# One core, a retention layer and a wave-MLP: the whole program behind the first loads in another order

## The chip, the cores and the metric

The kernel runs on one core of a Trainium2 chip. The metric is the device time of one execution in microseconds (us). The kernel before takes 165.86 us, the median of 3 runs (165.68 to 165.93). The core's engines are told apart by the names that the profile gives them: PE (TensorE, with PEld for its weight loads), DVE (VectorE), ACT (ScalarE), POOL (GpSimd), and SP (SyncE), which here only issues DMAs. Each engine takes its instructions from its own queue, in program order.

## The reference

For 4 batches, 8 heads, 768 tokens and a head size of 64 the first half is a recurrence with a decay gamma per head. Its output, laid out as 4 x 768 x 512, is the input of the second half.

```
state = gamma * state + k[t] (outer) v[t]          # per batch and head, 64 x 64
x[t]  = (q[t] @ state) / sqrt(64)
theta = x @ w_theta                                # 512 x 512
y     = w_tok_r @ (x * cos(theta)) + w_tok_i @ (x * sin(theta))   # 768 x 768, per batch
u     = x + y
out   = u + max(u @ w_ch, 0)                       # 512 x 512
```

All tensors in memory are 32 bit; the kernel multiplies in bf16.

## The kernel before, in words

The recurrence is done in blocks. A unit n (0 to 23) is 256 tokens of 4 heads of one batch: six units to a batch, units n and n+1 (n even) being the two head groups of the same tokens. A chunk C or t (0 to 23) is 128 tokens of all heads, six to a batch. The second half needs all six chunks of a batch, since w_tok_r and w_tok_i mix tokens.

There are no loops in the program's order. A text, ORDER (lines 22 to 86), is a list of tokens such as `Lk.4.a`: a step, a unit or chunk, at times a second index, and where there is a choice the engine or queue (`v` DVE, `a` ACT, `p` POOL, `s` SP). The last loop of the kernel (line 603) calls the steps one by one. The list alone fixes the order in every engine's queue. Semaphores between the engines, and the buffers that a tile gets, come from the framework. Loads, stores and transposes that SP and ACT issue are counted in program order on eight semaphores in turn, so that such a DMA is not issued before the one eight places ahead of it has landed.

The steps of a unit n:

- `Lk`, `Lq`, `Lv` (line 157): load k, q or v of the unit, 256 KB each, from SP's or ACT's queue. There are 16 buffers for k and q together and 9 for v.
- `ck`, `cq` (lines 137, 139): cast k or q to bf16. `cqs` (302) does the cast of q and multiplies by the decay of its token at once; where `cq` is used, the decay comes in later, in `XA`. `cv` (308): cast v, with its decay.
- `Tk`, `Tq` (316): transpose k or q on PE, four blocks each, into PSUM; `E` (137, 139) copies both to SBUF. `Dk` (332) does the same by a DMA transpose that SP issues.
- `A` (346): the products of q and k, on PE; `m` (355): mask them, on DVE.
- `ST` (373): the unit's addition to the state, on PE; `S0`, `S1` (391, 395): add it to the running state; `SB` (139, 137): cast the state to bf16, in two halves.
- `I` (411) and `Y` (423): the state's and the products' part of the output, on PE, into the two PSUM banks R0 and R1 in which the next unit's `ST` also writes. There is one buffer of each, so `I` of unit n waits until `S0`, `S1` and both `XB` or `XA` before it have been read out.
- `XB` (137, 139): copy a chunk's half of the output as bf16 to the tile xT. `XA` (441): the same on DVE, multiplied by the decay qx.

The steps of a chunk: `Tx` (455) and `Ex`, or `Dx` (462): transpose xT to x, on PE with a copy or by DMA. `Hh` (469): theta. `CN` (476): cosine and sine, on ACT. `z` (483): x times both, on DVE or POOL. `M.t.s` (509): the two products of token block s for output chunk t, two matmuls of 512 columns. `u` (516): add x. `Tu` (521) and `Eu`, or `Du` (531): transpose u. `O` (536): the last product. `f` (542): relu and add. `SO` (547): store. `Mh`, `uh`, `Tuh`, `Euh`, `Oh`, `fh`, `SOh` do the last chunk in two halves.

The weights: `Pth`, `Pch` and `Pw.r.g` (173, 176, 182) load them from POOL's queue, w_tok in three groups of rows each (1, 2 and 3 blocks). `Tw`, `Ew` (491, 137, 139) transpose w_tok. `const1` to `const9` make the constants; `const9` and `const8` are eight activations on ACT for qx (line 233), the later 512 and the first 256 tokens. `Z` (278) is a pair of matmuls on zeros.

Of the kernel before, what the change touches and what calls it, by code (L numbers as in the profile page):

```python
# [39 lines left out]
Tu.0 I.7 cv.8.p E.8.a cv.9.p Y.7 ST.8 A.8 cqs.9.v ck.9.v M.2.4 Du.1 Lk.10.s Eu.0.a XB.7.1.a XB.7.0.v  # L40
S0.8.v SB.8.0.v M.2.2 Tx.6 Tq.9 Tk.9 Lv.10.a cv.10.p ck.10.p Lq.10.s S1.8 u.2 m.8 O.0 E.9.a SB.8.1.a
Hh.6 Tw.1.4 I.8 Y.8 A.9 CN.6.0 Du.2 Lq.14.s CN.6.1 Ex.6.v f.0 ST.9 Tw.0.3 Hh.7 Ew.1.4.v Ew.0.3.a
S0.9.v Tw.0.4 M.3.0 Tw.1.5 CN.7.0 CN.7.1 M.3.2 Dx.7 M.3.1 M.3.5 M.3.3 Lv.12.s Lk.12.s Ew.1.5.v
XA.8.1 Ew.0.4.v Lq.12.s M.3.4 u.3 S1.9 Tw.0.5 Tk.10 M.4.5 cqs.10.p XA.8.0 m.9 M.4.3 Tq.10 SB.9.1.a
SB.9.0.a I.9 O.2 Lq.11.s Lk.11.s E.10.a Lk.15.s Ew.0.5.v Lk.14.s Y.9 ST.10 A.10 z.7.p Lv.11.s
# [588 lines left out]
```

## Time and profile before

| what | value |
|---|---|
| median of 3 runs | 165.86 us (165.68 to 165.93) |
| span of the profiled execution, first to last instruction | 164.0 us, 4889 instructions |
| PE busy | 153.7 us, 94% |
| DVE busy | 113.1 us, 69% |
| ACT busy | 79.6 us, 49% |
| POOL busy | 76.9 us, 47% |
| moved by DMA | 34.93 MB, mean 213 GB/s |

The page gives no other time for the profiled execution than its span; the 1.9 us between the span and the median of the runs lie outside the first and the last instruction. Busy time is an average over stages of unlike limits, and PE's end times are modelled. Rows of the views read: start in us, length in us, engine, line, operation, tiles written and read, and in brackets how long the engine sat idle before and what ended that. In grouped rows the figures behind the bar are the busy time in us and the mean length of one in ns.

### The profile page before, as it was taken

To read this page: it belongs to the slowest core of one execution; us is meant where nothing else is said; L and a number is where in the kernel's file an instruction comes from. 1 tells how busy PE (TensorE), PEld (TensorE's weight loads), DVE (VectorE), ACT (ScalarE), POOL (GpSimd) and SP (SyncE) were. 2 spreads that over 40 slices of the span, in tenths; PEclk is the share of its full clock that TensorE was granted. 3 is DMA by queue.
4 is the path that set the end of the run, shared out by engine and by line. 5 is a ranking of instruction groups with operands and counts; after the bars stand their busy time and mean duration, and the time that the engine had idled before them with its cause. 6 is when DMAs were issued, how large, how long until landed. Compare 5 with 4: busy or idle time off the path is not lost.

```text
span 164.0 us, 4889 instructions
## 1 busy us (share of the span) xinstructions
PE 153.7 (94%) x2001; PEld 87.0 (53%) x2030; DVE 113.1 (69%) x210; ACT 79.6 (49%) x142; POOL 76.9 (47%) x109
## 2 busy tenths in 40 slices
PE   5997789999999999999999999999999999999992
PEld 1455556656666655654454565555555545455550
DVE  3298677977993896994879895789867760244462
ACT  4976889983658245762433725832341616000020
POOL 7957279186306733730307599951469104500000
PEclk9999999999999999999999999999999999999999
DMA  4999999999999999949999896999999438514455
GB/s 118 297 290 251 272 284 250 279 217 280 210 214 257 290 170 222 310 115 285 318 259 199 173 247 182 187 169 301 213 271 131 96 83 211 160 68 123 104 209 203
DMA packets 69062, 34.93 MB, mean 213 GB/s; under 512 B 26416, under 2 KB 66096, under 8 KB 69040
## 3 DMA queue, kind: packets, MB, share of 16 engines
q1 hardware_dynamic: 56032, 23.73, 67.4%
q10 hardware_dynamic: 10320, 7.47, 16.1%
q0 software_dynamic: 2688, 3.41, 12.1%
q8 instruction: 16, 0.26, 0.7%
q14 instruction: 6, 0.05, 0.1%
HBM read 25.69 MB, written 6.29 MB: 195 GB/s over the span
## 4 chain that ended last, share of the span: by engine, by line
PE 73%; DMA 12%; ACT 5%; POOL 4%; issue 2%; DVE 1%; DVEq 0%; SPq 0%; POOLq 0%; ACTq 0%
PE y_ps L509 35%; PE o_ps L536 12%; PE th_ps L469 9%; DMA row<-in_moe_w_tok_i_dram 5%; DMA kqf<-in_k_dram 4%; DMA kqf<-in_q_dram 4%; PE r_ps L423 3%; ACT qx L233 3%; PE at_ps L346 2%; PE r_ps L411 2%; PE kq_ps L316 2%; PE w_ps L491 2%; PE y_ps L561 2%; PE r_ps L373 1%; PE u_ps L521 1%
## 5 line engine op out<-in xcount | busy, mean ns | idle before, releaser
L509 PE MATMUL y_ps<-z,wti 128*128 128x512 bf16 x131 | 49.6, 379 | 1.0 <-issue 1.0
L509 PE MATMUL y_ps<-z,wtr 128*128 128x512 bf16 x131 | 49.7, 379 | 0.3
L483 POOL TENSOR_TENSOR z<-cs,x_sb 128x1024 bf16<-128x1024 bf16 x12 | 25.4, 2124 | 17.6 <-DMA x_sb<-xT 10.0
L355 DVE TENSOR_TENSOR at<-at_ps,mask 128x1024 bf16<-128x1024 f32 x24 | 29.2, 1216 | 0.6 <-PE at_ps L346 0.5
L308 POOL TENSOR_TENSOR vb<-vf,vsc 128x512 bf16<-128x512 f32 x17 | 18.0, 1063 | 21.3 <-DMA vf<-in_v_dram 21.0
L542 DVE SCALAR_TENSOR_TENSOR ot<-o_ps,u 128x512 f32<-128x512 f32 x23 | 15.8, 688 | 12.9 <-PE o_ps L536 12.8
L469 PE MATMUL th_ps<-wth,xT 128*128 128x512 bf16 x88 | 23.9, 379 | 0.5
L516 DVE TENSOR_TENSOR u<-y_ps,x_sb 128x512 bf16<-128x512 f32 x23 | 15.8, 688 | 12.0 <-PE y_ps L509 11.9
L536 PE MATMUL o_ps<-wch,uT 128*128 128x512 bf16 x88 | 23.2, 379 | 0.4 <-issue 0.2
L476 ACT ACTIVATE cs<-th_ps,zerob 128x512 bf16<-128x512 f32 x24 | 16.4, 684 | 12.7 <-PE th_ps L469 8.2
L476 ACT ACTIVATE cs<-th_ps,halfpi 128x512 bf16<-128x512 f32 x24 | 16.3, 684 | 10.5 <-issue 4.3
L139 POOL CAST sbd<-s 64x256 bf16<-64x256 f32 (+1 forms) x21 | 10.0, 476 | 22.9 <-DVE s L391 20.5
L509 PEld LDWEIGHTS <-wtr 128*128 128x128 bf16 x138 | 13.5, 98 | 12.7
L509 PEld LDWEIGHTS <-wti 128*128 128x128 bf16 x138 | 13.5, 98 | 11.9 <-DVE wti L139 0.2
L137 ACT COPY kqT<-kq_ps 128x1024 bf16<-128x1024 bf16 x12 | 12.1, 1012 | 10.9 <-PE kq_ps L316 10.9
L137 ACT CAST kqb<-kqf 128x512 bf16<-128x512 f32 x17 | 10.2, 619 | 8.0 <-DMA kqf<-in_k_dram 7.2
L469 PEld LDWEIGHTS <-xT 128*128 128x128 bf16 x96 | 8.9, 98 | 8.3
L536 PEld LDWEIGHTS <-uT 128*128 128x128 bf16 x92 | 8.4, 98 | 8.6
L316 PE MATMUL kq_ps<-ident,kqb 128*128 128x128 bf16 x120 | 11.2, 219 | 0.4 <-ACT kqb L137 0.2
L278 PE MATMUL zz<-zero 128*128 128x512 bf16 x27 | 9.5, 481 | 2.0 <-DVE zero L192 1.9
L423 PE MATMUL r_ps<-at,vb 64*64 64x128 bf16 x384 | 10.0, 221 | 1.1 <-DVE at L355 1.1
L316 PEld LDWEIGHTS <-kqb 128*128 128x128 bf16 x120 | 8.2, 98 | 4.5 <-POOL kqb L139 0.6
(77 smaller groups left out, 204.6 us busy)
## 6 DMA issues: line engine op xcount, KB each, us to landing
vf<-in_v_dram SPq DMA_DIRECT2D x20, 256.0 KB, 6.0
kqf<-in_k_dram SPq DMA_DIRECT2D x19, 256.0 KB, 5.3
kqf<-in_q_dram SPq DMA_DIRECT2D x17, 256.0 KB, 5.1
out_dram<-ot ACTq DMA_DIRECT2D x12, 256.0 KB, 3.0
out_dram<-ot SPq DMA_DIRECT2D x11, 256.0 KB, 3.1
kqf<-in_q_dram ACTq DMA_DIRECT2D x7, 256.0 KB, 5.4
kqf<-in_k_dram ACTq DMA_DIRECT2D x5, 256.0 KB, 5.0
vf<-in_v_dram ACTq DMA_DIRECT2D x4, 256.0 KB, 6.1
```

Source lines behind the costliest of these rows:

```text
L137: nc.scalar.copy(dst, src)
L308: engines[e].tensor_mul(in_blocks(vb), by_token(raw["vf", n]), _bcast_last(K["vsc"][:, i, :, h * HU:(h + 1) * HU], D))
L316: nc.tensor.transpose(st["kq_ps", n][:, 4 * w + x, :], st["kqb", n][:, w, x * P:(x + 1) * P], K["ident"])
L355: nc.vector.tensor_mul(at.rearrange("p g j a t -> p (g j) (a t)"), st["at_ps", n].rearrange("p g j a t -> p (g j) (a t)"), _bcast_mid(K["m ...
L423: nc.tensor.matmul(st["R", n + 1][c][g * D:(g + 1) * D, j * P:(j + 1) * P], st["vb", n][rows, lo:lo + D], st["at", n][rows, g, j, a, :], s ...
L469: nc.tensor.matmul(th_ps, st["xT", C][:, j, :], K["wth"][:, j, :], start=(j == 0), stop=(j == 3))
L476: nc.scalar.activation(st["cs", C][:, w, :], st["th_ps", C], AF.Sin, bias=K["zerob" if w else "halfpi"], scale=1.0)
L483: engines[e].tensor_mul(st["z", b][:, c], st["cs", C], _bcast_mid(x_of(C), 2))
L509: nc.tensor.matmul(st["y", t], K["wT"][r][:, s0, t0 * P:(t0 + 1) * P], st["z", b][:, s0, r, :], start=(done == 0 and r == 0), stop=(done = ...
L516: nc.vector.tensor_add(st["u", t], st["y", t], st["x", b][:, t0, :])
L536: nc.tensor.matmul(o_ps, st["uT", t][:, j, :], K["wch"][:, j, :], start=(j == 0), stop=(j == nD - 1))
L542: nc.vector.scalar_tensor_tensor(st["ot", t], st["o", t], 0.0, st["u", t], ALU.max, ALU.add)
```

## The change

Only ORDER is changed. The first 17 tokens (constants, the first five loads) stay as they are. Behind them nearly every step stands in another place, although units and chunks are still worked off in the same succession. What else differs:

- Casts and copies. `E` on DVE goes from 3 to 7 of 15, on ACT from 12 to 8. `z` on DVE goes from 12 to 16 of 24, on POOL from 12 to 8. q is scaled in its cast in 16 units instead of 13 (`cqs`), so that `XA` falls from 22 to 16 and `XB` rises from 26 to 32; but units 0 to 3, which had `cqs`, now have `cq` and `XA`. `ck` goes on DVE from 5 to 2, on POOL from 7 to 9, on ACT from 12 to 13. `Ew` has 8 on DVE (9) and 4 on ACT (3).
- Queues. Of 72 loads ACT issues 30 (16 before) and SP 42 (56 before); of the stores ACT issues 11 in place of 12, the last half chunk aside.
- Transposes. Chunk 8 has `Dx` for `Tx` and `Ex`, and `Du` for `Tu` and `Eu`. As the diff has it these are two transposes more by DMA; the nine `Dk` are the same.
- In the first part: `Lk.1` goes from SP to ACT's queue, behind `const9`. `Lq.4`, `Lk.4` are issued ahead of `const8` instead of behind it, `Lv.5` by ACT. `Pw.1.0`, `Pw.0.0`, `Pw.0.1`, `Pw.1.1` follow on POOL behind `ck.5` and `cv.5`, with no `z` between them.

The diff, cut to its beginning (up to `M.1.1`) and its end:

```diff
 ORDER = """
-const2 Lv.0.s const1 const6.v Z.29 Z.2 const5 Z.38 Lk.0.a const3 Z.35 Z.8 Lq.0.s Lv.1.s Z.28 constA
-const4 Lq.1.a cqs.0.v const9 Lk.1.s cv.0.p Z.39 const8 ck.0.p Tk.0 Tq.0 ck.1.a E.0.v Lq.4.a ST.0
-Lk.4.a Z.15 A.0 cqs.1.p Tq.1 Lq.2.s S0.0.v SB.0.1.v Lk.2.s SB.0.0.p cv.1.p Lv.2.s S1.0 I.0 Z.27 m.0
-Tk.1 E.1.a Y.0 ST.1 XB.0.1.a cqs.2.v Z.34 S0.1.v S1.1 cv.2.p SB.1.0.a Pth Lq.3.s Z.18 XB.0.0.v Tq.2
-A.1 SB.1.1.a ck.2.a Tk.2 const7 I.1 Z.23 m.1 Y.1 XB.1.0.a Lk.3.s E.2.v XB.1.1.v A.2 ck.3.p m.2 ST.2
-S0.2.v S1.2 SB.2.1.a Z.11 cqs.3.p Tq.3 Lv.3.s Tx.0 Tk.3 Z.3 ck.4.p Lv.4.s Lk.5.s Lq.5.s Lv.5.s
-Lq.6.s Lk.6.s Lv.6.s Lq.7.s E.3.a SB.2.0.v I.2 Y.2 XB.2.1.a Ex.0.a cv.3.v cq.4.p Tk.4 Lq.8.s A.3
-ST.3 Lk.7.s S0.3.v SB.3.0.a S1.3 Lv.7.s Lk.8.s Tx.1 Tq.4 SB.3.1.p cv.4.p m.3 Pw.1.0 XB.2.0.a Ex.1.a
-I.3 Lv.8.s E.4.a cq.5.a Y.3 Pw.0.0 ST.4 Hh.0 ck.5.a S0.4.v XB.3.0.v XB.3.1.v cv.5.v CN.0.1 A.4
-CN.0.0 Tq.5 Hh.1 Tk.5 SB.4.0.p SB.4.1.a Pw.0.1 Hh.2 m.4 E.5.v I.4 Y.4 ST.5 ck.6.a Tk.6 Tx.2 cq.6.a
-CN.1.1 CN.1.0 XA.4.1 A.5 XA.4.0 m.5 Lq.9.s Ex.2.v S0.5.v z.0.p Tq.6 E.6.a CN.2.0 cv.6.p Hh.3
-SB.5.0.v Tx.3 Tw.1.0 z.1.v SB.5.1.a Ew.1.0.v Ex.3.a CN.2.1 A.6 I.5 Y.5 ST.6 XA.5.0 z.2.v Tw.0.0
-CN.3.0 Tx.4 CN.3.1 Ew.0.0.v S0.6.v XA.5.1 Ex.4.v Hh.4 CN.4.0 CN.4.1 Tw.0.1 M.0.1 Pw.1.1 z.3.v M.0.0
-Tw.0.2 Pw.1.2 Ew.0.2.a SB.6.1.a Hh.5 z.4.p SB.6.0.p Lk.9.a M.0.3 ck.7.p cqs.7.p M.0.2 CN.5.1 CN.5.0
-cq.8.a m.6 Ew.0.1.v Tw.1.1 Tw.1.2 Ew.1.1.v Lv.9.s M.0.4 M.1.0 Tx.5 Ew.1.2.v M.1.1 S1.6 Tk.7 M.1.4
...
-M.20.5 u.20 O.22 Mh.1.5 uh.1 f.22 Tu.20 SO.14.a SO.19.s Eu.20.a O.21 SO.18.a Tuh.1 Euh.1 f.21 O.20
-f.20 Oh.0 Oh.1 SO.21.a SO.22.s SO.20.s fh.0 SOh.0 fh.1 SOh.1 Z.31
+const2 Lv.0.s const1 const6.v Z.29 Z.2 const5 Z.38 Lk.0.a const3 Z.35 Z.8 Lq.0.s Lv.1.s Z.28 constA const4
+Lq.1.a cq.0.v const9 cv.0.p cq.1.v ck.0.p Tk.0 Lk.2.s Lk.1.a Tq.0 Z.18 ST.0 Z.39 Lq.4.a Lq.2.s E.0.v Lv.2.s
+Lq.5.s S0.0.v Lk.3.s A.0 Tq.1 SB.0.1.v cv.1.v Lk.4.a const8 ck.1.a Lv.3.s Tk.1 S1.0 Lq.3.s ck.2.a SB.0.0.v
+Z.15 Lv.4.s Lk.5.s m.0 I.0 cq.2.a Y.0 cv.2.p Pth E.1.v XA.0.1 A.1 cqs.4.v ST.1 Tk.2 Z.3 cq.3.p S0.1.v Z.34
+Tq.2 m.1 ck.4.a E.2.v Lq.6.s XA.0.0 Tq.4 ck.3.a cq.5.p A.2 Z.27 SB.1.0.v S1.1 SB.1.1.a I.1 m.2 cv.3.p Y.1
+const7 ST.2 Lk.7.s XA.1.0 cv.4.p ck.5.p S0.2.v Tk.3 XA.1.1 Tk.4 Tq.3 Z.11 S1.2 Lk.6.s Z.23 E.3.v A.3
+SB.2.0.a Lv.5.a Tx.0 SB.2.1.a I.2 Y.2 E.4.v ST.3 Tx.1 m.3 S0.3.v Ex.1.v Lq.7.s Tq.5 XA.2.1 Pw.1.0 XA.2.0
+Lv.6.s SB.3.1.a S1.3 SB.3.0.a A.4 cv.5.p I.3 Y.3 ST.4 Pw.0.0 Hh.0 m.4 CN.0.0 Ex.0.v XA.3.0 Pw.0.1 XA.3.1
+S0.4.v Tk.5 CN.0.1 E.5.v Tx.2 Ex.2.v Pw.1.1 Hh.1 SB.4.0.a CN.1.0 SB.4.1.v Lq.8.s Hh.2 I.4 ck.6.p Y.4 ST.5
+cqs.6.v Tq.6 Lk.8.s A.5 z.0.v CN.1.1 Hh.3 S0.5.v SB.5.1.a SB.5.0.a Tk.6 CN.2.1 Tw.1.0 XB.4.0.v XB.4.1.v I.5
+m.5 Pw.1.2 E.6.a cv.6.v Lv.7.a Y.5 A.6 ST.6 z.1.v CN.2.0 Ew.1.0.a XA.5.0 Tw.0.0 Tx.3 Ew.0.0.v z.2.p Ex.3.v
+CN.3.1 m.6 Hh.4 S0.6.v CN.3.0 Tx.4 M.0.0 z.3.p Tw.0.2 M.0.1 Lk.9.a Ex.4.a Lv.9.a Ew.0.2.v CN.4.1 M.0.2
+Lk.10.a Tw.0.1 SB.6.0.a CN.4.0 XA.5.1 ck.7.p Ew.0.1.a Tx.5 Lv.10.a z.4.v Ex.5.a Lv.8.s S1.6 Hh.5 Tw.1.1
+CN.5.0 CN.5.1 SB.6.1.p M.0.4 Tw.1.2 cq.7.p M.0.3 Ew.1.1.v Tk.7 I.6 z.5.v Ew.1.2.a M.1.0 cv.7.v Tq.7 E.7.a
+Lq.9.s M.1.1 cqs.8.p M.1.2 M.0.5 Lk.18.a M.1.4 Pch Tq.8 Y.6 Pw.0.2 A.7 ST.7 ck.8.v u.0 Tw.1.3 Tk.8 S0.7.v
...
+Mh.1.4 M.20.1 Mh.1.3 Tuh.0 f.18 M.20.2 Du.21 M.20.0 u.20 O.22 Mh.1.5 Tu.20 SO.18.s Euh.0 f.22 uh.1 Eu.20.a
+O.21 SO.16.a Tuh.1 f.21 Euh.1 SO.22.a O.20 SO.21.a Oh.0 Oh.1 f.20 Z.31 SO.20.a fh.0 fh.1 SOh.0 SOh.1
 """.split()
```

More of the change, by code (lines that the diff above doesn't have):

```diff
@@ L40 @@
[L40 to L45, printed above, removed]
@@ new lines @@
+M.8.4 M.8.1 XB.13.1.v Lq.21.a cv.15.v S0.14.v Dk.16 M.8.0 cqs.18.p Lq.19.s XB.13.0.a Lv.20.s SB.14.1.p
+Lk.19.a M.8.2 Hh.13 CN.13.0 Dk.17 u.8 Tx.12 S1.14 M.10.0 M.10.4 SB.14.0.p M.10.5 Du.7 CN.13.1 I.14 Hh.12
+SO.4.s Y.14 m.15 ST.15 A.16 S0.15.v M.10.3 XB.14.0.v S1.15 SB.15.1.p CN.12.0 M.10.2 CN.12.1 Lk.21.s
+XB.14.1.v O.6 ck.20.a M.10.1 Dx.13 SB.15.0.p I.15 Y.15 m.16 ST.16 ck.21.a A.17 f.6 cqs.20.p u.10 O.7 S0.16.v
+XB.15.0.v Dk.18 M.11.1 Lv.19.s XB.15.1.v cv.18.p ck.19.p SB.16.1.a Tx.15 M.11.3 Du.10 Ex.12.a SB.16.0.a I.16
```

76 lines of the change are left out of this document (36 added, 40 removed).

## The prediction

> **What bounds the kernel now.** I read the page's engine table first, then the same by stages, then the chain of waits of the first 40 us, and only then single instructions. The table:
>
> ```profile
> PE 153.7 (94%) x2001; PEld 87.0 (53%) x2030; DVE 113.1 (69%) x210; ACT 79.6 (49%) x142; POOL 76.9 (47%) x109
> ```
>
> PE is the bound on average. The stages (start and end in us, length, then each engine's busy time) and two matmuls of `M` in a row say where:
>
> ```profile
> 5.00:30.00 25.00, 22.09 (x427) 13.91 (x434) 18.15 (x35) 20.54 (x37) 17.54 (x23) 1.00 1.19 272
> 25.00:30.00 5.00, 4.78 (x108) 3.27 (x111) 3.92 (x9) 4.77 (x8) 4.12 (x4) 1.00 1.14 256
> 32.00:160.00 128.00, 125.72 (x1529) 70.39 (x1551) 90.66 (x165) 54.22 (x98) 55.62 (x56) 1.00 0.94 203
> ...
> 36.36 0.38 PE L509 MATMUL y_ps<-z,wtr 128*128 128x512 bf16 x1
> 36.58 0.38 PE L509 MATMUL y_ps<-z,wti 128*128 128x512 bf16 x1
> ```
>
> The columns behind the length are PE, PEld, DVE, ACT and POOL, then the granted clock, which is full. From 32 us on PE is busy 125.72 of 128 us, and its matmuls of 512 columns start 0.22 us apart: there it does nothing but its work, and an order can hardly win. From 5 to 30 us PE is busy 22.09 of 25 us, in pieces that often wait for one another, and DVE, ACT and POOL are at 70 to 82%; from 25 to 30 all four are near full. So the change is decided in the first 32 us, and by what it makes PE wait for later. The chain of waits shows what sets the front:
>
> ```profile
> 5.47 3.38 ACT qx L233 x6
> 9.27 6.62 DMA kqf<-in_k_dram
> 15.91 0.37 SPq L157
> 16.32 5.75 DMA kqf<-in_q_dram
> 24.53 1.17 POOL z L483
> 25.70 0.91 issue
> 26.61 0.98 POOL vb L308
> 27.60 8.04 DMA row<-in_moe_w_tok_i_dram
> ...
> 37.39 0.22 PE x_ps L455 x4
> 44.07 0.22 PE u_ps L521 x4
> ```
>
> ACT computes qx; only then does it reach `Lk.4.a`, at 9.27; the DMA eight places behind it, SP's `Lk.5`, may not go before that lands, at 15.91; q of unit 5, its casts, the cosine and `z.0` on POOL follow, and behind `z.0` and `cv.6` POOL asks for the weights `Pw.1.1`, at 27.60.
>
> **The change part by part.** *PE.* `Tx.8` and `Tu.8` go, two groups of four transposes at 0.22 each in the chain: **-0.45 us**, all of it on the path, since PE is dense there. Their copies `Ex.8` (DVE) and `Eu.8` (ACT) go too, into idle time. In their place SP issues `Dx.8` and `Du.8`, whose landing takes:
>
> ```profile
> uT<-u SPq DMA_TRANSPOSE x16, 3.2
> x_sb<-xT SPq DMA_TRANSPOSE x12, 3.6
> kqf<-in_k_dram ACTq DMA_DIRECT2D x5, 256.0 KB, 5.0
> ```
>
> In the new order PE has 15.9 us of work between the last `M.8` and `O.8`, counting each step by its pieces in the chain (0.43 for an `M`, 0.86 for `Hh` and `O`, 0.22 for four transposes). A transpose of 3.2 us hides there. If SP were late by 12 us it would not; in SP's queue `Du.8` stands right behind `Du.10`. `Dx.8` stands behind `Dk.12`, with 17 us of PE's work up to the first `M` that needs it.
>
> *Loads.* ACT issues 14 loads more. The nearest row is an issue beside a running copy: the copy begins at 33.81, the issue at 33.82, and the next copy at 34.63 without a pause.
>
> ```profile
> 33.81 0.80 ACT L137 COPY wtr<-w_ps 128x768 bf16<-128x768 bf16 x1 [0.36 <-PE w_ps L491]
> 33.82 0.38 ACTq L157 DMA_DIRECT2D kqf<-in_k_dram  x1
> 34.63 0.29 ACT L137 CAST sbd<-s 64x128 bf16<-64x128 f32 x1
> ```
>
> So I take 0; were each on the path it would be 14 x 0.38 = 5.3 us, and ACT has 84 us idle. The one that counts is `Lk.1`. It went out from SP's queue early enough that `ck.1` at 8.79 waited for ACT alone; now ACT reaches it when the last of `const9`'s four activations has begun.
>
> ```profile
> 8.79 0.62 ACT L137 CAST kqb<-kqf 128x512 bf16<-128x512 f32 x1
> 3.96 4.89 ACT L233 ACTIVATE qx<-pos,lscale,lgp 128x512 f32<-128x512 f32 x8 [0.43 <-POOL lgp L228]
> L233 ACT ACTIVATE qx<-pos,lscale,lgp 128x512 f32<-128x512 f32 x4 | 2.9, 802 | 0.4 <-POOL lgp L228 0.4
> 12.13 0.39 PE L316 MATMUL kq_ps<-ident,kqb 128*128 128x128 bf16 x4
> 12.92 1.23 DVE L355 TENSOR_TENSOR at<-at_ps,mask 128x1024 bf16<-128x1024 f32 x1 [0.36 <-PE at_ps L346]
> ```
>
> That is 3.96 + 2.9 - 0.8 = about 6.1. It lands some 5.0 later, at 11.1; `ck.1` on ACT takes 0.62 (to 11.7), `Tk.1` 0.39 (12.1), and `E.1`, now on DVE, 0.68 (12.8). Nothing on DVE passes `E.1`: behind it wait `XA.0.1`, `cqs.4` and `S0.1`, 1.2 together, and then `m.1`, at 14.0. In the kernel before `m.1` began at 12.92.
>
> *Casts and copies in the first units.* Through `m.5` DVE has 45 instructions in place of 30: three `E`, four of `XA` and `XB`, three `Ex`, two `cq`, two `SB`, one `z` and one `S0` more, one `cv` less. Their rows, and three instructions in a row that show the spacing:
>
> ```profile
> L139 DVE COPY kqT<-kq_ps 128x1024 bf16<-128x1024 bf16 x3 | 2.1, 684 | 1.2 <-PE kq_ps L316 1.2
> L137 ACT COPY kqT<-kq_ps 128x1024 bf16<-128x1024 bf16 x12 | 12.1, 1012 | 10.9 <-PE kq_ps L316 10.9
> L441 DVE TENSOR_TENSOR xT<-r_ps,qx 128x256 bf16<-128x256 f32 x22 | 8.7, 416 | 1.8 <-PE r_ps L373 1.8
> L139 DVE CAST kqb<-kqf 128x512 bf16<-128x512 f32 x6 | 2.9, 501 | 0.0
> L483 DVE TENSOR_TENSOR z<-cs,x_sb 128x1024 bf16<-128x1024 bf16 x12 | 8.2, 682 | 0.2
> 22.95 0.69 DVE L308 TENSOR_TENSOR vb<-vf,vsc 128x512 bf16<-128x512 f32 x1
> 23.56 1.22 DVE L355 TENSOR_TENSOR at<-at_ps,mask 128x1024 bf16<-128x1024 f32 x1
> 24.69 0.68 DVE L139 COPY kqT<-kq_ps 128x1024 bf16<-128x1024 bf16 x1
> 27.17 1.22 DVE L355 TENSOR_TENSOR at<-at_ps,mask 128x1024 bf16<-128x1024 f32 x1
> 29.57 0.40 PE L411 MATMUL r_ps<-kqT,sbd 128*128 128x128 bf16 x4
> ```
>
> By length: 3 x 0.68 + 7 x 0.42 (`Ex` as long as `XA`) + 2 x 0.50 + 2 x 0.3 + 0.68 + 0.3 - 0.69 = 6.9 (0.3 stands for the small casts and sums of the state, after the one of 0.29 on ACT above); an instruction follows the one before it 0.08 earlier than that one's length (22.95 to 23.56), so 15 x 0.08 less: **5.7 us** more. ACT loses three `E` of 1.01 in the same part. From `m.1` at 14.0 up to `m.5` the new queue holds 31 instructions, by the spacing 4 x 1.13 (`m`) + 4 x 0.60 (`E`) + 12 x 0.34 (`XA`, `XB`, `Ex`) + 9 x 0.2 (states) + 2 x 0.60 (`cqs`, `z`) = 14.0. If DVE never waited, `m.5` would begin at 28.0, where it began at 27.17 before: 0.8 later. If it waited as much as before, 5.7 later. It idled 6.85 of the 25 us from 5 to 30, and this would shrink to 1.1. I take it that DVE, with more work ready, keeps about a third of the 4.9 us between these ends, so that `m.5` comes 0.8 + 1.5 = 2.3 us later. Some 1.2 of this is slack: `m.5` was done at 28.4, and `I.5` and `Y.5` behind it only began at 29.57. What is left is **+1.1 us** (from 0 to 4.5) at the place where PE gets dense.
>
> *POOL.* It does four `z` fewer, and `Pw.1.1` stands ahead of both its `z`. But `Pw.0.0` to `Pw.1.1` stand behind `cv.5`, whose load ACT issues behind `SB.2.0`. I put this between 2 us for and 1 us against, and take 0, since PE was already busy 4.78 of 5 us before the rows came.
>
> *After 32 us.* DVE stays some 5 us ahead in work, of 37 that it idles there; POOL hands it four more `z`. I take **+0.3** for waits on `m` and `u` (0 to 1.5). One more matter is contention between DVE and POOL:
>
> ```profile
> 86.72 2.03 POOL L308 TENSOR_TENSOR vb<-vf,vsc 128x512 bf16<-128x512 f32 x2
> 87.20 2.10 DVE L302 TENSOR_TENSOR kqb<-kqf,qsc 128x512 bf16<-128x512 f32 x1
> L302 DVE TENSOR_TENSOR kqb<-kqf,qsc 128x512 bf16<-128x512 f32 x6 | 5.6, 931 | 3.2 <-DMA kqf<-in_q_dram 3.2
> ```
>
> Six `cqs` took 5.6 us, 1.5 more than six of the 0.68 that I take for an undisturbed one; one beside POOL's `cv` took 2.10. From 39 instructions of DVE on SBUF alone the new order goes to 42, so this costs 0.1 more; it lies within the +0.3. [...]
>
> Sum, against the profiled span of 164.0: +1.1 - 0.45 + 0.3 = +0.95, so 164.95; with the 1.86 us by which the median of the runs (165.86) stands above this span, **166.8 us**.
>
> **The rivals.** *Faster.* `Lk.4` now goes out ahead of `const8`, whose four activations take 4.89 - 2.9 = 2.0, so some 2.0 before 9.27; the chain's pieces from `z.0` to `cv.6` (1.17 + 0.91 + 0.98) no longer stand before `Pw.1.1`; and ACT, 4.77 of 5 us busy from 25 to 30, is freed. If the front is set by this chain and DVE's waits were only its shadow, the front moves 2.0 earlier and the time is 165.86 - 2.0 - 0.45 = 163.4. It decides if `m.5` begins before 27.2. Against it: DVE cannot reach `m.5` before 28.0 by its own work, unless `E.1` comes earlier than 12.1.
>
> *DVE becomes the bound of the front.* If it keeps all its waits, `m.5` is 5.7 later and the front 4.5: 165.86 + 4.5 - 0.45 = 169.9. Speaking for it: its waits come from PE and loads in turn. Against: part of its idle time is waiting for `E` copies that ACT took 1.01 for and DVE takes 0.68 for.
>
> *No difference.* The front's delay is eaten by the slack before `I.5`, and only the transposes count, with some later waits: 165.5 to 166.2.
>
> **How the numbers follow.** I call a difference under 0.2% (0.33 us) none, about what a measurement here can tell. Forecast, later front by 0.5 to 2.5 us net: 0.42. DVE as the bound, above 168.4: 0.13. No difference: 0.13. Faster, 163.2 to 165.5: 0.32. So faster 0.32, same 0.13, slower 0.55. The likeliest case's own range is 166.2 to 168.4. The range for 8 in 10 takes in most of the faster case and the milder part of the DVE case: 164.0 to 168.8.
>
> **What would show it.** Right: `Lk.1` issued at about 6.1 and `E.1` on DVE past 12; `m.1` near 14; DVE over 4.4 of each 5 us from 15 to 35; `m.5` past 28; from 35 us on PE as dense as before, with its work of the end in the same distances. Wrong: `m.5` before 27.2, or PE dense before 30 us; or gaps of PE over 0.5 us behind 40 us, at `O`, `A` or `Hh`, which would be DMA transposes or loads that I costed at nothing.

## The result and the profile after

The changed kernel takes **172.57 us**, the median of 4 runs (172.14 to 173.19), against 165.77 us (165.61 to 165.93) for the kernel before on the same chip: a ratio of 1.042 (95% interval 1.039 to 1.0445), 6.9 us slower by the ratio. The forecast was 166.8, at most 168.8. All ratios leave out executions over 1.5% above the fastest of their kernel; of experiments 1 and 5 these are two of four each (in experiment 1 172.50 and 172.87 us, beside 169.64 and 170.30).

Line numbers of the changed kernel are 5 lower than before's (`M` is L504, `Hh` L464, `CN` L471, `O` L531, `I` L406, loads L152), and those of most lists in the experiments 6 lower. First the page's table of engines and the chain's shares, then the same stages as in the prediction, with the same columns:

```profile
PE 156.2 (92%) x2022; PEld 86.1 (51%) x2022; DVE 118.4 (70%) x219; ACT 73.3 (43%) x134; POOL 69.4 (41%) x106
...
PE 69%; DMA 12%; DVE 8%; ACT 3%; issue 2%; POOL 1%; SPq 1%; ACTq 1%; DVEq 0%; POOLq 0%
```

```profile
5.00:30.00 25.00, 21.34 (x390) 12.14 (x388) 22.48 (x46) 14.51 (x27) 12.78 (x18) 1.00 1.16 270
25.00:30.00 5.00, 3.99 (x66) 1.99 (x64) 4.94 (x10) 3.25 (x7) 4.14 (x6) 1.00 0.98 212
32.00:160.00 128.00, 123.47 (x1531) 67.73 (x1524) 89.41 (x159) 53.04 (x99) 52.27 (x58) 1.00 0.93 199
```

Up to 30 us it is as forecast: DVE is full from 25 to 30 us (4.94 of 5), and PE is a little less busy, 21.34 us for 22.09. The surprise stands in the last row. Behind 32 us PE was to stay dense; it is busy 2.25 us less than before in the same 128 us. The waits of PE from 33 to 42 us, and then from 90 to 112 us, name the places (time in all, how often, the longest):

```profile
PE th_ps L464 <- ACT cs L471: 2.2, 1, 2.2
...
PE o_ps L531 <- ACT cs L471: 1.1, 1, 1.1
PE r_ps L406 <- ACT sbd L132: 1.0, 1, 1.0
```

To place the loss I use **PE's delay**: the start of a step on PE, less the work of all of PE's steps ahead of it in the list, each counted by its pieces in the chain of waits (0.43 us an `M`, 0.86 an `Hh` or `O`, 0.35 a `Y`, 0.22 four transposes). It grows only where PE waits or runs slower. Read at these times (us):

| kernel | 32 | 40 | 98 | 120 | 160 |
|---|---|---|---|---|---|
| before | 10.2 | 10.7 | 10.9 | 11.1 | 11.2 |
| changed | 11.9 | 14.8 | 14.9 | 17.2 | 17.3 |

The steps are: up to 36 us 1.75 (12.4 for 10.65); **2.37 at `Hh.5`**, at 38.72; **1.13 at `I.16`**, at 100.52; **1.24 at `O.8`**, at 108.13. Behind the last full output tile 0.65 more are lost (5.2 us from its start to the end, 4.5 before). With 0.45 us less work on PE this makes 6.7; the spans differ by 6.3.

The largest step, `Hh.5`, in ACT's time line:

```profile
34.29 0.58 ACT L132 COPY x_sb<-x_ps 128x512 bf16<-128x512 bf16 x1 [0.39 <-PE x_ps L450]
34.30 0.37 ACTq L152 DMA_DIRECT2D vf<-in_v_dram  x1
34.74 3.00 ACTq L152 DMA_DIRECT2D kqf<-in_k_dram  x1
34.77 0.69 ACT L471 ACTIVATE cs<-th_ps,zerob 128x512 bf16<-128x512 f32 x1
37.79 0.30 ACT L132 CAST sbd<-s 64x128 bf16<-64x128 f32 x1 [2.32 <-issue]
...
37.99 0.68 ACT L471 ACTIVATE cs<-th_ps,halfpi 128x512 bf16<-128x512 f32 x1
```

`Lv.9` is issued in 0.37 us, `Lk.10` behind it in 3.00, with the same 256 KB. While ACT's sequencer stands in it, the engine has nothing to do ("2.32 <-issue"). `CN.4.0`, behind it, starts at 37.99 and frees the PSUM bank of `Hh.5`. It is no wait for the DMA eight places ahead: that was `Lv.5`, landed at 25.71. Nor is it one for a buffer: the one 16 places ahead, of `Lk.2`, had been read by 10.9 us. Over both traces, an issue of a load with none of its own queue's DMAs on the way took 0.41 us on average (15 of them), with three on the way some 0.65 (25, `Lk.10` among them), with five or more 1.1 to 1.2 (at least 22, at most 3.34). So the number on the way is not all. From the DMA view, the three loads of ACT's queue (q10) that were ahead of `Lk.10` had hardly moved: 13 packets from 30.45 to 34.74 us, where one load is some 530, while the rows of w_tok from POOL's queue (q0) took most of the 16 DMA engines' time (86.4%). While the issue stood, to 37.74 us, q10 moved 265, and from then to 42 us, in the second view, 1660 (the columns are packets, MB, and the share of the 16 engines' time):

```profile
q0 software_dynamic: 446, 0.66, 86.4%
q1 hardware_dynamic: 520, 0.26, 27.5%
q10 hardware_dynamic: 13, 0.01, 0.5%
```

```profile
q10 hardware_dynamic: 1660, 0.82, 68.3%
q0 software_dynamic: 216, 0.31, 39.8%
```

In the kernel before the long ones, 2.81 and 2.49 us, were all SP's, which computes nothing.

### The profile page after: what moved, and what is told of

Read it like the earlier page. It is cut to its first block, busy times and chain, and to the rows that moved or that the text cites. A ratio compares the mean times of both kernels' runs of the same rounds, so it can differ in the third digit from the quotient of the medians.

```text
span 170.3 us, 4901 instructions
## 1 busy us (share of the span) xinstructions
PE 156.2 (92%) x2022; PEld 86.1 (51%) x2022; DVE 118.4 (70%) x219; ACT 73.3 (43%) x134; POOL 69.4 (41%) x106
## 3 DMA queue, kind: packets, MB, share of 16 engines
q0 software_dynamic: 2688, 3.41, 11.6%
## 4 chain that ended last, share of the span: by engine, by line
PE 69%; DMA 12%; DVE 8%; ACT 3%; issue 2%; POOL 1%; SPq 1%; ACTq 1%; DVEq 0%; POOLq 0%
PE y_ps L504 33%; PE o_ps L531 11%; PE th_ps L464 9%; DMA kqf<-in_q_dram 5%; DMA kqf<-in_k_dram 4%; PE r_ps L418 3%; DMA kqT<-kqb 3%; PE kq_ps L311 2%; PE at_ps L341 2%; PE w_ps L486 2%; PE r_ps L406 2%; PE y_ps L556 2%; DVE xT L436 1%; DVE at L350 1%; DVE z L478 1%
## 5 line engine op out<-in xcount | busy, mean ns | idle before, releaser
L504 PE MATMUL y_ps<-z,wtr 128*128 128x512 bf16 x138 | 52.4, 380 | 0.0
L504 PE MATMUL y_ps<-z,wti 128*128 128x512 bf16 x138 | 52.3, 379 | 0.0
L464 PE MATMUL th_ps<-wth,xT 128*128 128x512 bf16 x96 | 24.7, 379 | 2.6 <-ACT cs L471 2.2
L303 POOL TENSOR_TENSOR vb<-vf,vsc 128x512 bf16<-128x512 f32 x18 | 19.5, 1085 | 18.5 <-DMA vf<-in_v_dram 18.4
L471 ACT ACTIVATE cs<-th_ps,halfpi 128x512 bf16<-128x512 f32 x24 | 16.5, 688 | 23.9 <-PE th_ps L464 19.9
L531 PE MATMUL o_ps<-wch,uT 128*128 128x512 bf16 x92 | 23.6, 380 | 1.1 <-ACT cs L471 1.1
L511 DVE TENSOR_TENSOR u<-y_ps,x_sb 128x512 bf16<-128x512 f32 x23 | 15.9, 690 | 12.4 <-PE y_ps L504 12.0
L478 POOL TENSOR_TENSOR z<-cs,x_sb 128x1024 bf16<-128x1024 bf16 x8 | 17.4, 2179 | 11.0 <-ACT cs L471 10.3
L504 PEld LDWEIGHTS <-wtr 128*128 128x128 bf16 x138 | 13.5, 98 | 12.9
L504 PEld LDWEIGHTS <-wti 128*128 128x128 bf16 x138 | 13.5, 98 | 12.2
L471 ACT ACTIVATE cs<-th_ps,zerob 128x512 bf16<-128x512 f32 x24 | 16.4, 684 | 4.7 <-PE th_ps L464 4.4
L478 DVE TENSOR_TENSOR z<-cs,x_sb 128x1024 bf16<-128x1024 bf16 x16 | 12.3, 782 | 7.7 <-ACT cs L471 5.3
L134 POOL CAST sbd<-s 64x256 bf16<-64x256 f32 (+1 forms) x19 | 7.2, 378 | 22.0 <-DVE s L386 16.4
L464 PEld LDWEIGHTS <-xT 128*128 128x128 bf16 x96 | 8.9, 97 | 11.9 <-issue 2.9
L134 POOL CAST kqb<-kqf 128x512 bf16<-128x512 f32 x13 | 8.1, 626 | 12.4 <-PE r_ps L368 6.0
L531 PEld LDWEIGHTS <-uT 128*128 128x128 bf16 x92 | 8.4, 98 | 9.2 <-issue 1.2
L311 PE MATMUL kq_ps<-ident,kqb 128*128 128x128 bf16 x120 | 11.2, 222 | 1.9 <-POOL kqb L134 0.8
L132 ACT COPY kqT<-kq_ps 128x1024 bf16<-128x1024 bf16 x8 | 8.1, 1010 | 10.9 <-PE kq_ps L311 10.8
L132 ACT CAST sbd<-s 64x256 bf16<-64x256 f32 (+1 forms) x22 | 8.3, 378 | 10.0 <-DVE s L386 7.4
L273 PE MATMUL zz<-zero 128*128 128x512 bf16 x30 | 10.4, 481 | 1.9 <-DVE zero L187 1.9
```

The source lines that it names most:

```text
L132: nc.scalar.copy(dst, src)
L134: engines[e].tensor_copy(dst, src)
L303: engines[e].tensor_mul(in_blocks(vb), by_token(raw["vf", n]), _bcast_last(K["vsc"][:, i, :, h * HU:(h + 1) * HU], D))
L311: nc.tensor.transpose(st["kq_ps", n][:, 4 * w + x, :], st["kqb", n][:, w, x * P:(x + 1) * P], K["ident"])
L464: nc.tensor.matmul(th_ps, st["xT", C][:, j, :], K["wth"][:, j, :], start=(j == 0), stop=(j == 3))
L471: nc.scalar.activation(st["cs", C][:, w, :], st["th_ps", C], AF.Sin, bias=K["zerob" if w else "halfpi"], scale=1.0)
```

## The experiments

All edits are in ORDER. "Above before" is (ratio - 1) x 165.7 us, with the 95% interval; the changed kernel stands at 6.9 (6.5 to 7.4). Executions of one list with the stall at `Hh.5` scatter by up to 4.5 us (169.84 to 174.35 in experiment 5), so of these lists I read PE's delay at a place rather than the time.

**1. Two loads off ACT's queue.**

```diff
-Lk.10.a ... Lv.10.a ... Lq.9.s
+Lq.9.s Lk.10.s Lv.10.s
```

> The changed kernel with two loads, Lk.10 and Lv.10, taken from ACT's queue and given to SP's, directly behind Lq.9, so that they still go out while the rows of w_tok and four other loads are under way. Theory A (the issue on ACT is the cost): in the changed kernel ACT sat 3.00 us in the issue of Lk.10 at 34.74, the sine of chunk 4 behind it came late, and the PSUM bank for Hh.5 with it. Then Hh.5 starts without the stall of 2.37 us, SP shows the long issue instead, and the time falls by 2.0 to 2.4 us, to about 170.3. Rival B (the queues are full because of the traffic, and whatever waits for data or for DVE would hold Hh.5 anyway): PE still stands for 1.5 us or more between 36 and 39 us, and the time stays within 0.5 us of 172.57.

Ratio 1.027 (1.024 to 1.030): **4.4 us above before (3.9 to 4.9)**, 2.5 gained, read from two executions of four. In the trace `Hh.5` has no stall; ACT goes on:

```profile
34.31 0.69 ACT L470 ACTIVATE cs<-th_ps,zerob 128x512 bf16<-128x512 f32 x1
34.89 0.29 ACT L131 CAST sbd<-s 64x128 bf16<-64x128 f32 x1
35.08 0.68 ACT L470 ACTIVATE cs<-th_ps,halfpi 128x512 bf16<-128x512 f32 x1
```

Theory A holds for the place and, in these two executions, for the size; only SP's two issues, at 28.51 and 29.57, were not long here (0.96 and 1.04).

**2. The converse: four loads on ACT in the kernel before.**

```diff
-CN.4.0 CN.4.1 ... Lk.9.a ... Lv.9.s ... Lk.10.s ... Lv.10.a
+CN.4.0 Lv.9.a Lk.9.a Lk.10.a Lv.10.a CN.4.1
```

> The kernel before with four loads, Lv.9, Lk.9, Lk.10 and Lv.10, issued by ACT one behind the other between CN.4.0 and CN.4.1, at about 33.5 us, while the rows of w_tok are under way; before, two of the four were SP's, and ACT's two stood behind CN.4. Theory A (an engine that issues a load while several of its own queue are on the way stands in the issue until one has moved): one of the four issues takes 2 us or more, CN.4.1 comes late by that and by four issues, Hh.5 or the copies of w_tok stop PE for 1 to 3 us near 36 us, and the time is 166.8 to 168.5. Rival B (it was the changed kernel's late front, not the issue): every issue takes under 1 us, and the time stays within 0.6 us of the kernel before.

Ratio 1.033 (1.031 to 1.035): **5.5 us above before**, more than either theory said.

```profile
32.46 1.08 ACTq L151 DMA_DIRECT2D kqf<-in_k_dram  x2
33.58 2.77 ACTq L151 DMA_DIRECT2D vf<-in_v_dram  x1
36.39 0.69 ACT L470 ACTIVATE cs<-th_ps,zerob 128x512 bf16<-128x512 f32 x1 [3.67 <-issue]
```

The fourth load stands 2.77 us, and `Hh.5` loses 3.67. The rest, about 1.5 us by my estimate, is PE's clock behind the pause, 0.63 from 36 to 39 us and 0.81 from 39 to 42 (last section). So an issue that stands, on an engine that computes, is enough by itself, with no late front. Here too ACT's queue hardly moved while it stood: 42 packets from 33.58 to 36.35 us, with POOL's rows at 84.8% of the engines' time.

**3. The casts ahead of `SB.16`.**

```diff
-ck.20.a ... ck.21.a ... SB.16.1.a Tx.15 M.11.3 Du.10 Ex.12.a SB.16.0.a
+SB.16.1.a Tx.15 M.11.3 Du.10 Ex.12.a SB.16.0.a ck.20.a ck.21.a
```

> The changed kernel with the casts ck.20 and ck.21 moved on ACT from ahead of SB.16.1 to behind SB.16.0; nothing else. Theory A: ACT stood 2.99 us at ck.21 for the load Lk.21, which SP had issued only at 93.49, and both halves of SB.16 came late, so that I.16 lost 1.13 us at 100.52. Then this stall goes, and the time falls by 1.1 us, to about 171.5; if the wait of 1.24 us at O.8, 108.13, is only the echo of it (Hh.15 and Hh.14 come late, and the buffer of cosines with them), it goes too, and the time falls by 2.4 us, to about 170.2. Rival B: I.16 is held by S0, S1 or the reading of the output's banks as well, and the gain is under 0.4 us.

5.9 us above before (4.7 to 7.2). The time alone would not settle it; in the trace the stall at `I.16` is gone, and `O.8` still waits 1.39. So `I.16` was ACT standing at `ck.21` for a load that SP had issued late:

```profile
98.41 0.62 ACT L132 CAST kqb<-kqf 128x512 bf16<-128x512 f32 x1 [2.99 <-DMA kqf<-in_k_dram]
...
99.03 0.40 ACT L132 CAST sbd<-s 64x256 bf16<-64x256 f32 x1
```

(ACT's time line of the changed kernel.) And `O.8` is no echo of it: it waits although `I.16` no longer does.

**4. `z.15` on DVE.**

```diff
-z.15.p
+z.15.v
```

> The changed kernel with z.15 on DVE in place of POOL; nothing else. Theory A: the wait of 1.24 us at O.8 comes from POOL's z.15, which took 2.58 us (104.20 to 106.78) and held the buffer of cosines for which CN.14 waited 3.45 us, and CN.14 held the PSUM bank of O.8. Then O.8 starts without a wait, and the time falls by about 1.2 us, to 171.4. Rival B (z.13 and z.15 are late because their x is late, that is, because of the DMA transposes Dx.13 and Dx.14 or the stall at I.16): DVE then waits for x, u and m queue behind it, and the gain is under 0.4 us or a loss.

7.2 us above before (6.2 to 8.1): no gain in the time. In the trace the wait at `O.8` is gone, 0.49 comes back at `Hh.17`; the profiled execution lost 1.6 us to PE's clock behind `Hh.5`, 0.52 from 39 to 42 us (last section). The cause of the wait at `O.8` is shown, its worth is not. The row of the changed kernel that held the buffer of cosines:

```profile
104.20 2.58 POOL L478 TENSOR_TENSOR z<-cs,x_sb 128x1024 bf16<-128x1024 bf16 x1
```

**5. The last stores.**

```diff
-SO.22.a ... SO.20.a
+SO.22.s ... SO.20.s
```

> The changed kernel with the stores SO.22 and SO.20 issued by SP in place of ACT, as in the kernel before; nothing else. Theory A: of the time lost, 0.65 us lies behind the last full output tile, since ACT issues four stores one behind the other (2.29 us for three of them) and the last half chunk's store waits for its turn. Then the end moves 0.3 to 0.65 us earlier, to 171.9 to 172.3. Rival B: the end is set by the transfer of the last store alone, which shares the DMA engines with the others whoever issues them, and the change is under 0.2 us.

The time (4.9 above before, 4.1 to 5.7) can't show an edit of the last 8 us here. In the trace the stretch from `fh.1` to the end is 4.0 us, against 4.2 in the changed kernel and 3.5 before: rival B, it is not who issues the stores. The likely cause is that `SO.16` now goes out among the last (163.34, before 141.10): in the traces of experiments 8 and 9, where it goes out earlier, the stretch is 3.4 to 3.6. It is not shown, since the first list of experiment 10, with `SO.16` still among the last, has 3.5.

**6. Half the list from each kernel.** Up to `Ex.3` (32 us) from the changed one, the rest from before; and up to `I.6` (40 us) from before, the rest changed.

```diff
+list 6a: changed kernel up to Ex.3, then what is left in before's order
+list 6b: kernel before up to I.6, then what is left in the changed order
```

> The changed kernel's list up to Ex.3, about the first 32 us, and behind it everything that is left in the order of the kernel before. Theory A (the loss is in separate places, and the front's is the prediction's): the front's delay of 1.1 predicted, 1.75 read from the trace, and nothing else: about 167.3 (166.7 to 167.8), PE's delay grown by 1.3 to 2 us at 36 us and unchanged from there on. Rival B (the front's delay is eaten by slack): within 0.4 us of the kernel before. Rival C (the late front itself sets off the later waits at Hh.5, I.16 and O.8): 169.5 or more.

> The list of the kernel before up to I.6, about the first 40 us, and behind it everything that is left in the changed order (units 6 and 8 keep the cast cq, and so XA, unit 7 cqs and XB). Theory A: what is left of the loss is I.16 (1.1), O.8 (1.2) and the tail (0.5), less 0.45 for chunk 8: about 168 (167.4 to 168.8), with PE as dense as in the kernel before up to 95 us. Rival C (the later waits are echoes of the late front): within 0.6 us of the kernel before, since nothing is late at 40 us. Rival D (the later order is bad throughout): PE falls behind in many small steps between 45 and 95 us, and the time is 169.5 or more.

Both cost **4.2 us above before** (3.7 to 4.7 and 3.4 to 5.0), 8.4 together, where the whole costs 6.9. That doesn't show that the two overlap, since each half also has a wait of its own that the changed kernel has not (1.44 and 1.11, below).

- 6a: PE's delay is 13.2 at 36 us, 2.5 more than before, and 1.44 more are lost at `M.0.5`, at 43.40; from 46 us on it is flat. Neither A nor C in full: the late front alone gives no wait at `I.16` or `O.8`, but it does more than its own 1.75. At `M.0.5` DVE's `z` of chunk 5, beside POOL, took 2.62 us in place of 0.68, and the `cv` behind it 1.52:

```profile
40.72 2.62 DVE L477 TENSOR_TENSOR z<-cs,x_sb 128x1024 bf16<-128x1024 bf16 x1
43.27 1.52 DVE L302 TENSOR_TENSOR vb<-vf,vsc 128x512 bf16<-128x512 f32 x1
```

- 6b: the waits at `I.16` (1.43) and `O.8` (1.24) are there without a late front; C falls. A new 1.11 at `Tw.0.3` is my splice's own: five loads fell together on ACT, and the fifth stood 4.40 us.

**7. The transposes of chunk 8 alone, in the kernel before.**

```diff
-Dk.12 Tx.8 ... Ex.8.v ... Du.10 ... Tu.8 ... Eu.8.a
+Dk.12 Dx.8 ... Du.10 Du.8
```

> The kernel before with chunk 8's transposes by DMA: Dx.8 behind Dk.12, Du.8 behind Du.10, without Tx.8, Ex.8, Tu.8 and Eu.8; nothing else. The prediction's step: PE does two groups of four transposes less, 0.45 us, and SP's transposes are hidden: about 165.2, PE's delay unchanged. Rival: the two DMA transposes hold up what SP issues behind them, or come late at Hh.8 or O.8, and the time is 166 or more with a gap of PE there.

Ratio 0.9998 (0.9983 to 1.0013), 10 runs: **no difference**. The 0.45 us that PE saves don't arrive, and nothing is lost. In the trace `I.18` loses 0.44, waiting for POOL's cast of the state, where it loses 0.22 in the kernel before; where the rest goes is not placed.

**8. Four edits together**, and on top of them one more at a time: three copies back on ACT; `Lv.5` on SP; with `Lv.5` on SP, the loads beside the rows of w_tok thinned out; and with these, `Lk.1` on SP.

```diff
+8a: edits 1, 3 and 4, and SO.16.s behind SO.17.s
+8b: 8a, and E.2.a E.3.a E.4.a for E.2.v E.3.v E.4.v
+8c: 8a, and Lk.5.s Lv.5.s for Lv.5.a behind SB.2.0
+8d: 8c, and Lk.10.a behind E.7, Lv.10.a behind E.8, Lk.18.a behind Lk.12, Lk.11.s behind Du.2
+8e: 8d, and Lk.1.s Lk.2.s for Lk.2.s Lk.1.a
```

> The changed kernel with four edits behind the first 32 us: Lk.10 and Lv.10 on SP behind Lq.9; ck.20 and ck.21 behind SB.16.0; z.15 on DVE; the store SO.16 on SP behind SO.17 instead of in the row of last stores. Theory A (separate places, each worth what the trace shows): 172.57 - 2.4 - 1.1 - 1.2 - 0.4 = about 167.5 (166.9 to 168.2), what is left against the kernel before being the front's 1.75 less 0.45 for chunk 8. Rival B (take one wait away and the next late tile stops PE a little further on, as M.0.5 did with the changed front on the old order): 169 or more, with a new gap of PE of over 0.7 us behind 40 us.

> The same four edits, and E.2, E.3 and E.4 on ACT in place of DVE, as in the kernel before. Theory A (the prediction's: DVE's extra work makes the front late): DVE is relieved of 3 x 0.68 = 2.0 us between 12 and 25 us, PE's delay at 32 us falls by 0.5 to 1 us, and the time with it, to 0.5 to 1 us below that of the four edits alone. Rival B (late loads and POOL's queue make the front late): PE's delay at 32 us falls by less than 0.2 us, or grows, since ACT takes 1.01 us for each and issues Lv.5 later still.

> The same four edits, and the load Lv.5 issued by SP behind Lk.5, in place of ACT behind SB.2.0. Theory B (late loads and POOL's queue): Lv.5 goes out near 14 instead of at 17.74 and lands some 3 us earlier than 25.7; cv.5 on POOL and the four requests for the rows of w_tok behind it follow, ck.6 no longer starts at 29.3, the wait of 0.82 us at Tk.6 goes, and the time falls by 0.5 to 1.2 us below that of the four edits alone. Theory A (DVE's work): cv.5 and the rows come earlier, but m.5 stays past 28.3 and the time changes by less than 0.3 us.

> The kernel with the four edits and Lv.5 on SP, and the loads thinned out while the rows of w_tok are under way: Lk.10 and Lv.10 on ACT only behind E.7 and E.8, Lk.18 behind Lk.12, Lk.11 on SP behind Du.2. Theory (the loads bunched between 28 and 42 us cost twice: they stop the engine that issues them, and they make the rows late): Pw.0.2 lands some 2 us or more earlier than 50.6, the wait of 1.16 us at Tw.0.3 goes, and the time falls from 167.65 to 166.3 to 166.9. Rival (the rows are late because POOL asks for them late, at 38.9): Pw.0.2 lands within 1 us of 50.6, Tw.0.3 still waits about 1 us, and the time stays within 0.4 us of 167.65.

> The same as the kernel with the rows alone, and Lk.1 issued by SP ahead of Lk.2 in place of ACT behind const9. The prediction's step: the load on ACT behind const9 makes ck.1, E.1 and m.1 late and so the front. Then Tk.1 loses its wait of 0.8 us at 10.3, PE's delay at 32 us falls by 0.4 to 0.8 us, and the time by as much. Rival: the front is set later, by Lv.5, POOL's queue and the copies E and Ex, or Lk.2 now lands late in its place: PE's delay at 32 us and the time change by less than 0.25 us.

| list | above before (interval) | delay at 32 | 40 | 98 | 160 |
|---|---|---|---|---|---|
| 8a | 3.1 (2.4 to 3.7) | 11.2 | 13.6 | 14.2 | 15.5 |
| 8b | 3.8 (3.2 to 4.4) | 12.1 | 12.8 | 13.6 | 15.3 |
| 8c | 2.0 (1.5 to 2.5) | 11.0 | 11.0 | 12.8 | 13.6 |
| 8d | 2.3 (1.8 to 2.9) | 11.0 | 11.0 | 12.5 | 13.2 |
| 8e | 2.8 (2.3 to 3.4) | 11.4 | 11.4 | 13.8 | 14.9 |

8a gains 3.8, not 5.1: rival B, in part. With `Hh.5` on time PE ran into the next late tile, a row of w_tok that landed at 38.32 (in the changed kernel at 37.21, hidden by the stall at `Hh.5`):

```profile
38.37 0.51 PE L485 MATMUL w_ps<-ident,row 128*128 128x128 bf16 x6 [1.69 <-DMA row<-in_moe_w_tok_i_dram]
```

8c takes this wait away as well as the one at `Tk.6`. `Lv.5` lands at 23.17 instead of 25.71, and POOL, which stood behind it, asks for the rows 3 us earlier. POOL's time line, of the changed kernel and then of 8c:

```profile
25.86 1.49 POOL L303 TENSOR_TENSOR vb<-vf,vsc 128x512 bf16<-128x512 f32 x1 [4.57 <-DMA vf<-in_v_dram]
27.30 1.32 POOL L177 DMA_DIRECT2D row<-in_moe_w_tok_r_dram  x2
```

```profile
23.32 1.03 POOL L302 TENSOR_TENSOR vb<-vf,vsc 128x512 bf16<-128x512 f32 x1 [2.13 <-DMA vf<-in_v_dram]
24.31 1.32 POOL L176 DMA_DIRECT2D row<-in_moe_w_tok_r_dram  x2
```

In 8d the last group of rows, `Pw.0.2`, lands at 48.72 (50.58 in 8c), and the wait of 1.16 at `Tw.0.3` goes, as the theory said; but 0.68 is lost at `I.11` instead and the time is no better. 8e is a miss: `Lk.1` from SP lands at 9.06, not 9.64, and `ck.1` starts no earlier (9.85; 9.78 in the changed kernel), since on ACT it stands behind `const8`:

```profile
7.65 2.07 ACT L228 ACTIVATE qx<-pos,lscale,lgp 128x256 f32<-128x256 f32 x4 [0.77 <-DMA kqf<-in_q_dram]
9.78 1.79 ACT L132 CAST kqb<-kqf 128x512 bf16<-128x512 f32 x3
```

(The changed kernel.) 8b does not test DVE's load cleanly: on ACT `E.2` stood behind a cast that waited 3.00 us for its load, `A.2` lost 2.0 us (0.7 in 8a), and behind this pause PE ran at half the clock from 17.46 to 20.87 us (the execution's mean clock is 0.99; last section). It shows only that these copies had no better place there.

**9. The old front with the edits of the later part, and three edits of that.**

```diff
+9a: kernel before up to I.6, then 8d's order, with Lk.10.a behind ST.7
+9b: 9a, and Tx.8 Hh.8 ... Ex.8.v ... Tu.8 Hh.14 Eu.8.a for Dx.8 and Du.8
+9c: 9a, and Dx.16 ahead of Dk.20, z.16.v for z.16.p
```

> The list of the kernel before up to I.6, about 40 us, and behind it the changed order with all edits of the later part (ck.20 and ck.21 behind SB.16.0, z.15 on DVE, SO.16 early, Lk.10 behind ST.7, Lv.10 behind E.8, Lk.18 behind Lk.12, Lk.11 on SP behind Du.2). Theory (the causes are separate and all found): nothing of the loss is left, chunk 8 brings up to 0.45 us: 165.2 to 166.0. Rival (the later order has more waits of its own): 166.5 or more, with a gap of PE behind 45 us that no run has shown yet.

> The kernel with the old front and the edits of the later part (168.77 us), and chunk 8's transposes back on PE: Tx.8, Ex.8 on DVE, Tu.8, Eu.8 on ACT in place of Dx.8 and Du.8. Theory A (PE is the bound, transposes by DMA are hidden): 0.45 us more work for PE, so 169.2. Theory B (in this order SP's queue, with eight DMAs under way at most, sets the pace between 50 and 110 us): two transposes of 1.2 us fewer on SP, what stands behind them goes out earlier, and the time falls by 0.4 us or more, to 168.4 or less.

> The kernel with the old front and the edits of the later part (168.77 us), with Dx.16 on SP ahead of Dk.20 and Du.9 instead of behind both, and z.16 on DVE in place of POOL, as in the kernel before. Theory: the wait of 0.87 us at M.13.4 (113.97) comes from z.16, whose x was asked for only at 106.28, behind two other transposes, and landed at 111.63; asked for near 104.6 it lands by 110, the wait goes, and the time falls by 0.5 to 0.9 us, to about 168.0. Rival: Dk.20 and Du.9, now later, stop PE at A.20 or O.9, and the time stays within 0.3 us.

9a was to leave nothing and is **3.2 us above before (2.6 to 3.8)**. PE's delay, 10.7 at 40 us as before, grows to 14.7 for the most part in six steps of 0.25 to 0.9 between 55 and 114 us: the later order has waits of its own, which had been covered in the changed kernel, where PE came 4 us later. **9b is 1.2 above before (0.8 to 1.5): two transposes back on PE, with 0.45 us more work for it, gain 2.0 us.** 9c, two edits in one, gains 1.0, and the wait at `M.13.4` is gone. In 9b SP's queue runs earlier (9a, then 9b):

```profile
61.70 3.26 SPq L326 DMA_TRANSPOSE kqT<-kqb  x1
65.05 1.22 SPq L456 DMA_TRANSPOSE x_sb<-xT  x1
66.32 0.57 SPq L151 DMA_DIRECT2D vf<-in_v_dram  x1
...
103.44 1.32 SPq L326 DMA_TRANSPOSE kqT<-kqb  x1
104.85 1.33 SPq L525 DMA_TRANSPOSE uT<-u  x1
106.28 1.26 SPq L456 DMA_TRANSPOSE x_sb<-xT  x1
```

```profile
61.30 3.31 SPq L326 DMA_TRANSPOSE kqT<-kqb  x1
64.67 0.57 SPq L151 DMA_DIRECT2D vf<-in_v_dram  x1
...
100.21 1.30 SPq L326 DMA_TRANSPOSE kqT<-kqb  x1
...
104.25 1.26 SPq L456 DMA_TRANSPOSE x_sb<-xT  x1
```

In 9a the issues follow one another: summed over 55 to 110 us, 46.3 of 55 us are issues (42 of them), in 9b 43.2, in the changed kernel 45.7, in the kernel before 33.2 (35 issues). A transpose holds SP 1.2 us and more (1.19 to 3.44 in the traces of the two kernels, median 1.22 and 1.24), a load mostly 0.4 to 0.8 (median 0.57 and 0.58). So `Lv.15` goes out 1.65 us later in 9a than in 9b, `Dk.20` 3.23 and `Dx.16` 2.03. `z.16`, and `M.13.4` behind it, waited for `Dx.16`. How much of the 2.0 us comes in this way is not shown: in 8d SP's issues take 44.9 of the 55 us, nearly as much, and there the same edit gains nothing (experiment 10).

**10. Chunk 8 back on PE in the changed kernel, and in 8d.**

```diff
-Dx.8 ... Du.8
+Tx.8 Hh.8 ... Ex.8.v ... Tu.8 Hh.14 Eu.8.a
```

> The changed kernel with nothing but chunk 8's transposes back on PE: Tx.8, Ex.8 on DVE, Tu.8, Eu.8 on ACT in place of Dx.8 and Du.8. Theory B (the two transposes crowd SP's queue): Lk.21 goes out about 1 us earlier than 93.49, the wait of 1.13 us at I.16 goes or shrinks to under 0.4, O.8 (whose buffer waits on the same chain) shrinks too, PE has 0.45 us more to do, and the time is 170.6 to 171.8. Theory A (the prediction's: hidden): the waits stay, and the time is 172.57 + 0.45 = 173.0.

> The kernel with the rows alone (168.21 us: the changed front with Lv.5 on SP, the four edits, the loads thinned out), and chunk 8's transposes back on PE. Theory B: as with the old front, where the same edit took 168.77 to 166.82, SP's queue runs 1 us or more earlier behind Dk.12, the wait at I.11 (0.68) and the small ones behind it go, and the time falls by 1 to 2 us, to 166.2 to 167.2. Theory A: 0.45 us more work for PE, 168.6.

6.3 (5.7 to 6.9) and 2.3 (2.0 to 2.6) above before. In the changed kernel `I.16` loses 0.60 in place of 1.13, `O.8` 1.02 in place of 1.24, but the time's intervals overlap, and in its trace PE comes some 3 to 4 us later there, which can shrink a wait by itself; in 8d the wait at `I.11` goes, PE's delay at 160 us falls from 13.2 to 12.5, and the time does not change. Neither theory as written. So the two transposes on SP cost between nothing and 2.0 us; what this depends on stays open, as SP's queue is about as full in 8d as in 9a. In none of four orders did they gain 0.45.

## Why the prediction was wrong

The direction was right; the time, and the place of most of the loss, were not. For the direction I had argued from the front alone, and most of the loss came from places that I had put at nothing or near it.

- **The step that failed first: "So I take 0" for ACT's 14 more loads.** The row that it leaned on was of ACT with few of its own loads on the way. One of the 14 took 3.00 us and PE 2.37 with it; without it the stall is gone and 2.5 us come back (experiment 1, two executions), and four loads in a row on ACT cost the kernel before 5.5 (experiment 2). The bound, 14 times 0.38, was wrong in kind: an issue had no fixed length here (0.37 to 3.34 us in the two kernels). "ACT has 84 us idle" was an average that said nothing of what stands behind the issue.
- **"After 32 us: +0.3 (0 to 1.5)" measured 4.7** (2.37, 1.13, 1.24). The last sign that I named for being wrong, gaps at `O`, `A` or `Hh` from transposes or loads costed at nothing, is what the trace shows, though the first of them stands at 38.7 us and not behind 40, and the gap at 100.5 is `I`.
- **-0.45 for chunk 8: refuted.** I had checked that the transposes land in time for their own readers, and not what stands behind them in SP's queue. Experiment 7 found no gain, 9b that they cost 2.0. (Up to the first `M` that needs `Dx.8`, `M.6.2`, the new list has about 12 us of PE's work and not 17; `Dx.8` landed 7 us before `M.6.2`, so this did no harm.)
- **The front: +1.1 forecast, 1.75 in the trace,** within the 0 to 4.5 given. `m.5` began at 28.68 (28.0 to 32.9 forecast). The size was nearly right, the cause only in part. `Lk.1` on ACT was issued at 4.79, not 6.1, `E.1` began at 11.36 and not past 12, `m.1` at 13.16 and not near 14, and moving `Lk.1` back gains nothing (8e). I had also misread its row: in the kernel before `Lk.1` landed at 8.76, 0.03 ahead of `ck.1`, so `ck.1` did not wait for ACT alone. POOL's step, costed at 0 between -2 and +1, was worth about 1 (8c, 1.1 below 8a): `Lv.5` on ACT held `cv.5` and the rows. How much DVE's 4.94 of 5 us contribute stays open; 8b could not tell. With `Lv.5` mended 0.8 us of delay are left at 32 us.
- **The tail, 0.65, was not in the sum.**
- **Contention of DVE and POOL: 0.1 within the +0.3.** In the changed kernel `z` on DVE takes 0.78 us on average (0.68 before), 16 x 0.1 = 1.6 us of DVE's time, most of it off PE's path; in list 6a a single `z` of 2.62 us stopped PE. Two of the changed kernel's 16 stand out, 1.53 us at 26.36 and 1.29 at 103.50, both with POOL busy throughout; the others took 0.68 to 0.77, also the one at 38.70 (0.77) beside a busy POOL. So a slowed `z` is rare here, but in 6a, where it was the next thing that PE needed, one instruction was enough (1.44 us at `M.0.5`).
- **Of the rivals** DVE as the bound came nearest in time (169.9), by another mechanism. "Faster" and "no difference" are out.

Of the 6.9 us the edits of 8c give back 4.9; 8c, 8d and the second list of experiment 10 all stay about 2 us above the kernel before. No list that was run beats it; experiment 7's equals it.

## What to carry to other kernels

Cost a DMA by the queue that issues it: look at what that engine has to compute next, how many DMAs of its own are on the way (here 0.41 us an issue with none, 1.1 to 1.2 with five or more), and what else stands behind it in that queue; an engine's idle share says nothing of this. When PE is late, later waits disappear, and when you mend the first stall they come back, so count a chain of stalls by removing them in order and not by adding up their rows. A transpose taken from a dense engine and given to a DMA queue saved its time in none of four orders here: look at what stands behind it in that queue.
